# Head-mix matmul as three float32r products for 76 of 180 blocks, with parts made on ScalarE and GpSimd

## The chip, the cores and the metric

One core of a Trainium2 chip runs the whole program. The metric is device time in microseconds, the median of several runs. In the profile PE is TensorE (matmuls; PEld is its weight loads), DVE is VectorE, ACT is ScalarE, POOL is GpSimd and SP is the engine that issues most DMA transfers. Each of them takes its own instructions in the order of the program, and waits only where one needs another's result or buffer.

## What is computed

Attention with two mixings over the heads, then a mixture of experts with one expert per token, then a feed-forward layer. Only the first part is touched by the change:

```python
scores = scale * np.matmul(q, k.transpose(0, 1, 3, 2))      # 4 x 12 x 448 x 448
scores = np.einsum('bhij,hg->bgij', scores, w_pre)          # head mix, 12 x 12
scores = scores - np.max(scores, axis=-1, keepdims=True)
attn = np.exp(scores)
attn = attn / (np.sum(attn, axis=-1, keepdims=True) + 1e-09)
attn = np.einsum('bhij,hg->bgij', attn, w_post)             # second head mix
out = np.matmul(attn, v)
```

All of it is float32. What follows (`_moe_ref`, `_moe2_ref`) reads the attention's output.

## The kernel before

The queries are cut into 16 tiles `T` (four per batch, of 120, 120, 120 and 88 rows). The scores of a tile (function `emit_S`, two head pairs at a time as `emit_S2`) are left in SBUF as `ssb`, rows by query. To mix heads, a matmul must contract over heads, so the tile is cut into 180 blocks in all, of 10 queries x 12 heads = 120 partitions (a few of 8 x 12 = 96). A DMA, `emit_relay`, moves each block from `ssb` into its own tile `sr` (eight buffers), seven steps ahead of its use.

The main loop has one step per block. In step `s` it issues, in this order: the relay for a later block; the head mix of block `s` (`emit_P`: one float32 matmul of 120 x 448 with the block-diagonal weights `wpre`, into PSUM tile `P`, then VectorE's row maximum `mx`); `emit_W(s-1)`, by which VectorE turns the row sum of the block before into the scaled second mix `w`; one "fill" of TensorE (`emit_S2` scores of a coming tile, `emit_AV2` attention times values for a finished one, or transposes); ScalarE's exponential of block `s`, called `ex()`, which writes `p` and the row sum; a conversion step `conv_do` (three VectorE and three GpSimd instructions on a 128 x 256 piece of the feed-forward weights, tiles `ct` and `cm`, and a store) in some steps; and the second mix `emit_T(s-2)`, four float32 matmuls that need both `p` and `w` of block `s-2`, with their copy to `A` by ScalarE. `P` and `T` have two PSUM buffers each. The tables that say which fill falls into which step are fixed when the program is built; the steps with `emit_AV2` come about every fourth.

A float32 value is split elsewhere in this kernel into a high part, rounded to float32r, and a low part, the rest. A product is then three float32r matmuls, high by high, low by high and high by low; `emit_S`, the experts and the feed-forward layer all do this already. The head mix `P` and the second mix `T` are plain float32, which the trace shows as two instructions per matmul.

Of the kernel before, what the change touches and what calls it, by code (L numbers as in the profile page):

```python
# [8 lines left out]
F32 = mybir.dt.float32  # L9
F32R = mybir.dt.float32r  # L10
# [20 lines left out]
def body(ctx: ExitStack, tc, q, k, v, w_pre, w_post, emb, tau, w1, w2, win, wout, out):  # L31
    nc = tc.nc
    pe, act, dve, pool, sp = nc.tensor, nc.scalar, nc.vector, nc.gpsimd, nc.sync
    B, H, S, D = q.shape
# [19 lines left out]
    def ps(tag, nm):  # L54
        if len(PB) > 1:
            tag = {"a": "h", "b": "h"}.get(tag, "o")
        return psum[-1].tile([128, 512], F32, tag=tag, name=nm, bufs=PB[-1][tag])
# [72 lines left out]
    if True:  # L130
        cp = ctx.enter_context(tc.tile_pool(name="route", bufs=1, side="left"))
        aA = actx.enter_context(tc.tile_pool(name="attnA", bufs=1, side="right"))
        a2 = actx.enter_context(tc.tile_pool(name="attnC", bufs=1, side="right"))
        ap = bctx.enter_context(tc.tile_pool(name="attnB", bufs=1, side="left"))

        LAG = 2
        NSR = 8
        taub = cp.tile([128, 1], F32, name="taub")
        nat = {}
# [35 lines left out]
        pool.affine_select(dmask, dmask, pattern=[[-12, 10]], compare_op=ALU.is_ge, fill=0.0, base=0, channel_multiplier=1)  # L175
        pool.affine_select(dmask, dmask, pattern=[[12, 10]], compare_op=ALU.is_ge, fill=0.0, base=11, channel_multiplier=-1)
        wpre = a2.tile([120, 120], F32, name="wpre")
        wpost = a2.tile([120, 120], F32, name="wpost")

        def prep_w():  # L180
            v3 = lambda t, i: t.rearrange("p (a b) -> p a b", b=i)
            mb = dmask.rearrange("p (i o) -> p i o", o=1).to_broadcast([120, 10, H])
            pool.tensor_tensor(v3(wpre, H), mb, wr[:, 0:1, :].to_broadcast([120, 10, H]), op=ALU.mult)
            pool.tensor_tensor(v3(wpost, 10), dmask.rearrange("p (o i) -> p o i", o=1).to_broadcast([120, H, 10]),
                              wr[:, 1, :].rearrange("p (g o) -> p g o", o=1).to_broadcast([120, H, 10]), op=ALU.mult)
# [128 lines left out]
        s_sb = {}  # L314
# [25 lines left out]
        blocks = []  # L340
        for T in range(4 * B):
            n = IT[T % 4][1]
# [6 lines left out]
        NBK = len(blocks)  # L349
# [5 lines left out]
        sr = {}  # L355

        def emit_relay(i):
            T, r, m = blocks[i]
            t = a2.tile([120, S], F32, tag="sr", name=f"sr{i}", bufs=NSR)
            sp.dma_start(t[:12 * m, :], s_sb[T][qsl(T, r, m), :, :])  # L360
            sr[i] = t

        def qsl(T, r, m):
            nb = IT[T % 4][1] // 10
            return slice(r, r + nb * 9 + 1, nb) if r < nb else slice(10 * r, 10 * r + m)

        pj = {}

        def emit_P(i):
            n = 12 * blocks[i][2]  # L370
            t = sr.pop(i)
            pt = ps("b", f"P{i}")
            pe.matmul(pt[:n, :S], wpre[:n, :n], t[:n, :], start=True, stop=True)  # L373

            flush2()
            mx = a2.tile([120, 4], F32, tag="mx", name=f"mx{i}", bufs=5)
            dve.tensor_reduce(mx[:n, 0:1], pt[:n, :S], op=ALU.max, axis=AX.X, negate=True)  # L377
            p = a2.tile([120, S], F32, tag="p", name=f"p{i}", bufs=LAG + 1)
            pj[i] = (p, mx)
            return lambda: act.activation(p[:n, :], pt[:n, :S], AF.Exp, bias=mx[:n, 0:1], scale=1.0, accum_out=mx[:n, 1:2])  # L380
# [261 lines left out]
    with mctx:  # L642
# [321 lines left out]
        def at(pos, fn, *a):  # L964
            side.setdefault(int(pos), []).append((fn, a))
# [3 lines left out]
        def at_e(pos, fn, *a):  # L969
            pos = int(pos)  # L970
            while pos in eused:
                pos += 1
            eused.add(pos)
            at(pos, fn, *a)
            return pos
# [8 lines left out]
        def posAV(T, p):  # L984
            f, nb = first[T + 1], ntile[T + 1]
            return f + LAG + 1 + p * nb / 6

# [48 lines left out]
        kinds = lambda k: [x[0] for x in side.get(k, [])]  # L1036
# [7 lines left out]
        for j, st in enumerate(steps):  # L1044
# [2 lines left out]
            at(ld, conv_load, j, ap)  # L1047
            at(st, conv_do, j, ap)

        nxt = [0]  # L1050

        w1c = []
# [16 lines left out]
        def relay_to(i):  # L1069
            while nxt[0] <= min(i, NBK - 1) and blocks[nxt[0]][0] in sdone:  # L1070
                emit_relay(nxt[0])
                nxt[0] += 1
# [4 lines left out]
        def flush(tag=None):  # L1077
            keep = []
            while late:
                x = late.pop(0)  # L1080
                if tag in (None, x[0]):
                    y = x[1]()
                    if x[0] == "e" and callable(y):
                        late2.append((x[0], y))
                else:
                    keep.append(x)
            late.extend(keep)
            if tag:
                flush2(tag)
# [3 lines left out]
        def flush2(tag=None):  # L1093
            for x in late2[:]:
                if tag in (None, x[0]):
                    late2.remove(x)
                    x[1]()
# [39 lines left out]
        prep_w()  # L1137
        relay_to(NSR - 1)
        at_e(4, tr_en)
# [7 lines left out]
        for _ in pen:  # L1147
            pass
        for s in range(NBK + LAG + 6):
            todo = side.get(s, [])  # L1150
            fill = [x for x in todo if x[0] in PEF]
            for fn, a in todo:
                if fn in (load_q, load_k, load_v, conv_load, zero_fill):
                    fn(*a)
            flush()
            relay_to(s + NSR - 1)
            ex = emit_P(s) if s < NBK else lambda: None
            if 0 <= s - 1 < NBK:
                emit_W(s - 1)
            for fn, a in todo:  # L1160
                if fn is emit_R and a[1] in (0, 1, 3):
                    fn(*a)
            i = s - LAG
            on = 0 <= i < NBK
            fill.sort(key=lambda x: x[0] not in (emit_S, emit_S2, emit_AV2))
            if fill and fill[0][0] in (emit_S, emit_S2, emit_AV2):
                run_fill(*fill.pop(0))
            ex()
            for fn, a in todo:
                if fn is conv_do:  # L1170
                    fn(*a)
            if on:
                emit_T(i)
                T_mm(i, 0, NJ)
                flush("d")
            turns = [x for x in fill if x[0] in (tr_q, tr_k)] if on else []
            for fn, a in turns:
                flush("e")
                late2.append(("e", fn(*a)()))
            if on:  # L1180
                emit_TE(i)
            for x in fill:
                if x not in turns:
                    run_fill(*x)
            for fn, a in todo:
                if fn in (to_experts, first_gather) or fn is emit_R and a[1] in (2, 4, 5, 6):
                    fn(*a)
            for fn, a in todo:
                if fn is do1:
                    fn(*a)  # L1190
        flush()
        flush2()
        for k_ in side:
            assert k_ < NBK + LAG + 6

# [334 lines left out]
    with tc.If(again > 0):  # L1530
# [8 lines left out]
        with tc.tile_pool(name="again", bufs=1, reuse_waits="tile") as gp:  # L1539
            with tc.For_i(0, NT // XT, 1) as tx:  # L1540
# [5 lines left out]
                for j in range(QJ):  # L1546
# [5 lines left out]
                    for hf in range(2):  # L1552
                        pt = ps("c", f"yx{j}_{hf}")
# [7 lines left out]
                with tc.For_i(0, F2 // FG, 1) as gx:  # L1561
# [33 lines left out]
                    for j in range(QJ):  # L1595
                        sl = slice(j * QT, (j + 1) * QT)
                        for n0 in (0, 384):
                            pt = ps("c", f"ox{j}_{n0}")
# [33 lines left out]
```

## Time and profile before

| | us |
|---|---|
| median of 3 runs (1297.14 to 1297.43) | 1297.22 |
| the profiled execution, its own time | 1295.99 |
| its span, first to last instruction | 1294.1 |
| PE busy in the span | 1283.5 |
| DVE busy | 1003.8 |
| ACT busy | 747.7 |
| POOL busy | 489.4 |

The attention loop takes the span's first 500 us or so, the experts and the feed-forward layer the rest. The granted TensorE clock was 1.0 throughout, the upper of the two levels, 2.4 GHz. Times in the rows further down are microseconds from the span's start unless marked ns; in rows of groups, the number after the comma is the mean of one instruction in ns.

### The profile page before, as it was taken

Reading aid. Unit: us, or ns where it says so; the run is one execution under the profiler, and the core shown is the slowest. Engines: PE = TensorE matmul, PEld = TensorE weight load, DVE = VectorE, ACT = ScalarE, POOL = GpSimd, SP = SyncE. Lnnn points to the kernel's source line nnn. Section 1 sums busy time; section 2 is a strip of 40 time slices with the busy share of each in tenths; the row PEclk is TensorE's granted clock in tenths of the full one; section 3 lists DMA queues with packets and bytes.
Section 4 is the critical chain, followed back from the end, with each engine's and each line's share of the span. In section 5 each row is a group of like instructions: output and inputs, shape, how many; then the busy total and the mean of one; then the engine's idle time right before and its main releaser. Section 6 shows DMA issues by size and latency. Waiting matters only on the chain.

```text
span 1294.1 us, 24851 instructions
## 1 busy us (share of the span) xinstructions
PE 1283.5 (99%) x9072; PEld 1125.4 (87%) x9072; DVE 1003.8 (78%) x2168; ACT 747.7 (58%) x1513; POOL 489.4 (38%) x497
## 2 busy tenths in 40 slices
PE   9999999999999999999999999999999999999998
PEld 6777777777777778999999999999999999999997
DVE  5877877787878677788787676788888887888886
ACT  6767666666766665555544545765444556444432
POOL 1334423351344126333223222454644544444431
PEclk9999999999999999999999999999999999999999
DMA  7887665666557458778988876321211123111102
GB/s 172 268 267 214 199 204 152 200 202 192 160 168 223 147 157 301 262 264 250 268 245 259 265 241 210 105 86 49 86 58 65 49 99 122 50 50 49 50 25 88
DMA packets 153077, 210.95 MB, mean 163 GB/s; under 512 B 57686, under 2 KB 113158, under 8 KB 152950
## 3 DMA queue, kind: packets, MB, share of 16 engines
q1 hardware_dynamic: 149680, 195.37, 49.1%
q0 software_dynamic: 2480, 12.19, 2.7%
q8 instruction: 74, 1.21, 0.4%
q10 hardware_dynamic: 790, 1.74, 0.4%
q14 instruction: 53, 0.43, 0.1%
HBM read 135.71 MB, written 35.01 MB: 132 GB/s over the span
## 4 chain that ended last, share of the span: by engine, by line
PE 94%; DVE 2%; DMA 2%; ACT 1%; issue 0%; POOL 0%; SPq 0%; DVEq 0%; POOLq 0%
PE T L412 12%; PE P L373 10%; PE AV L430 6%; PE o L1454 6%; PE o L1452 6%; PE o L1453 6%; PE h L1418 6%; PE h L1417 6%; PE h L1416 6%; PE S L330 5%; PE ypi L706 3%; PE ypi L707 3%; PE ypi L705 3%; PE hi L729 3%; PE hi L730 3%; PE hi L731 3%
## 5 line engine op out<-in xcount | busy, mean ns | idle before, releaser
L412 PEld LDWEIGHTS T<-w,p 120*112 120x112 f32 (+1 forms) x1440 | 166.1, 177 | 59.5 <-issue 46.0
L122 POOL TENSOR_TENSOR cm<-cm,ct 128x256 f32<-128x256 f32 x96 | 70.7, 736 | 313.5 <-DVE ct L119 291.6
L412 PE MATMUL T<-w,p 120*112 120x120 f32 (+1 forms) x1440 | 185.0, 272 | 0.2 <-ACT p L380 0.2
L1399 POOL TENSOR_TENSOR gl<-th,gh 128x512 fp32r<-128x512 f32 (+1 forms) x64 | 77.5, 1211 | 241.1 <-ACT gh L1398 180.4
L373 PE MATMUL P<-sr,wpre 120*120 120x448 f32 x360 | 166.3, 544 | 1.0 <-DMA sr<-ssb 1.0
L380 ACT ACTIVATE p<-P,mx 120x448 f32<-120x448 f32 x180 | 114.1, 634 | 89.9 <-DVE mx L387 76.2
L1420 ACT ACTIVATE u<-h 128x512 f32<-128x512 f32 (+1 forms) x64 | 35.0, 547 | 204.1 <-PE h L1418 204.1
L1452 PE MATMUL o<-woh,gh 128*128 128x384 f32 x448 | 151.4, 338 | 0.0
L1454 PE MATMUL o<-woh,gl 128*128 128x384 f32 x448 | 150.4, 336 | 0.0
L1453 PE MATMUL o<-wol,gh 128*128 128x384 f32 x448 | 150.1, 335 | 0.0
L1458 DVE TENSOR_TENSOR acc<-acc,o 128x384 f32<-128x384 f32 x196 | 106.5, 548 | 47.2 <-PE o L1454 47.2
L377 DVE TENSOR_REDUCE mx<-P 120x1 f32<-120x448 f32 x180 | 111.6, 620 | 28.9 <-PE P L373 26.7
L120 POOL TENSOR_TENSOR cm<-craw 128x256 f32<-128x256 f32 x96 | 66.9, 697 | 112.8 <-DMA craw<-in_moe_w_in 59.2
L417 ACT COPY A<-T 112x480 f32<-112x480 f32 x180 | 102.3, 568 | 9.7 <-PE T L412 9.7
L729 PE MATMUL hi<-xhi,w1h 128*128 128x256 f32 x336 | 95.3, 283 | 0.0
L730 PE MATMUL hi<-xli,w1h 128*128 128x256 f32 x336 | 95.2, 283 | 0.0
L731 PE MATMUL hi<-xhi,w1l 128*128 128x256 f32 x336 | 95.2, 283 | 0.0
L705 PE MATMUL ypi<-w2hi,hhi 128*128 128x384 f32 x272 | 93.9, 345 | 0.0
L430 PEld LDWEIGHTS AV<-A,v 112*64 112x64 f32 x1536 | 73.9, 137 | 21.8 <-issue 10.7
L706 PE MATMUL ypi<-w2li,hhi 128*128 128x384 f32 x272 | 91.2, 335 | 0.2 <-DVE w2li L673 0.2
L707 PE MATMUL ypi<-w2hi,hli 128*128 128x384 f32 x272 | 91.2, 335 | 0.0
L121 POOL TENSOR_SCALAR cm<-cm 128x256 f32<-128x256 f32 x96 | 85.9, 895 | 8.4
(299 smaller groups left out, 3436.3 us busy)
## 6 DMA issues: line engine op xcount, KB each, us to landing
sr<-ssb SPq DMA_DIRECT2D x176, 210.0 KB
r<-in_moe_w SPq DMA_DIRECT2D x72, 384.0 KB
r<-in_moe_w SPq DMA_DIRECT2D x52, 512.0 KB
craw<-in_moe_w_in SPq DMA_DIRECT2D x48, 256.0 KB
craw<-in_moe_w_out SPq DMA_DIRECT2D x48, 256.0 KB
wor<-wo_d SPq DMA_DIRECT2D x16, 768.0 KB
raw<-wi_d SPq DMA_DIRECT2D x15, 768.0 KB
wi_d<-cm SPq DMA_DIRECT2D x48, 128.0 KB
```

What stands on the lines that cost most here:

```text
L373: pe.matmul(pt[:n, :S], wpre[:n, :n], t[:n, :], start=True, stop=True)
L412: pe.matmul(pt[:CP, c * n:(c + 1) * n] if m == 10 else pv[:, c], p[:n, c * CP:(c + 1) * CP], w[:n, :] if m == 10 else wv, start=True, stop ...
L430: pe.matmul(pt[64 * hh:64 * hh + 64, x * 120:x * 120 + n], vt[b, p + x][:, hh, c, :], A[T][:, c, 2 * (p + x) + hh, :n], start=c == 0, stop ...
L705: pe.matmul(pt[:, :384], a, wh[:, n0:n0 + 384], start=f == 0, stop=False)
L706: pe.matmul(pt[:, :384], a, wl[:, n0:n0 + 384], start=False, stop=False)
L707: pe.matmul(pt[:, :384], l, wh[:, n0:n0 + 384], start=False, stop=f == KF - 1)
L729: pe.matmul(pt[:, :256], wh[:, sl], xh[:, c, :], start=c == 0, stop=False)
L730: pe.matmul(pt[:, :256], wh[:, sl], xl[:, c, :], start=False, stop=False)
L731: pe.matmul(pt[:, :256], wl[:, sl], xh[:, c, :], start=False, stop=c == KD - 1)
L1452: pe.matmul(pt[:, :384], gh[:, sl], wo[0][:, f, n0:n0 + 384], start=f == 0, stop=False)
L1453: pe.matmul(pt[:, :384], gh[:, sl], wo[1][:, f, n0:n0 + 384], start=False, stop=False)
L1454: pe.matmul(pt[:, :384], gl[:, sl], wo[0][:, f, n0:n0 + 384], start=False, stop=f == GF - 1)
```

## The change

Steps with an `emit_AV2` fill (41 of them between step 12 and step 168) prepare blocks `s+2` and `s+3`; if the step also holds scores, `s+2` alone. That is 35 steps with two blocks and 6 with one, 76 blocks of 180. Preparing a block (`split_sr`) is one ScalarE copy of `sr` (120 x 448) into a new float32r tile `sh` with three buffers, the high part, and one GpSimd subtraction that leaves the low part in `sr`. The weights are split once, in step 2, by two VectorE instructions (`split_w`). The head mix of a prepared block is then three float32r products; the other 104 stay as they were. Nothing else is altered.

```diff
+        AHEAD = 2
...
+        wprs = [a2.tile([120, 120], F32R, name=f"wpr{t}") for t in "hl"]
...
-            t = a2.tile([120, S], F32, tag="sr", name=f"sr{i}", bufs=NSR)
-            sp.dma_start(t[:12 * m, :], s_sb[T][qsl(T, r, m), :, :])
+            t = a2.tile([120, S], F32R, tag="sr", name=f"sr{i}", bufs=NSR)
+            sp.dma_start(t.bitcast(F32)[:12 * m, :], s_sb[T][qsl(T, r, m), :, :])
...
+        def split_w():
+            dve.tensor_copy(wprs[0], wpre)
+            dve.tensor_sub(wprs[1], wpre, wprs[0].bitcast(F32))
+
+        def split_sr(i):
+            n = 12 * blocks[i][2]
+            sh[i] = ap.tile([120, S], F32R, tag="sh", name=f"sh{i}", bufs=3)
+            act.copy(sh[i][:n, :], sr[i].bitcast(F32)[:n, :])
+            pool.tensor_sub(sr[i][:n, :], sr[i].bitcast(F32)[:n, :], sh[i].bitcast(F32)[:n, :])
...
-            t = sr.pop(i)
+            t, h = sr.pop(i), sh.pop(i, None)
             pt = ps("b", f"P{i}")
-            pe.matmul(pt[:n, :S], wpre[:n, :n], t[:n, :], start=True, stop=True)
+            if h is None:
+                pe.matmul(pt[:n, :S], wpre[:n, :n], t.bitcast(F32)[:n, :], start=True, stop=True)
+            else:
+                pe.matmul(pt[:n, :S], wprs[0][:n, :n], h[:n, :], start=True, stop=False)
+                pe.matmul(pt[:n, :S], wprs[1][:n, :n], h[:n, :], start=False, stop=False)
+                pe.matmul(pt[:n, :S], wprs[0][:n, :n], t[:n, :], start=False, stop=True)
...
+        splits = {k: [k + AHEAD, k + AHEAD + 1][:1 if emit_S2 in kinds(k) else 2] for k in range(12, NBK - 11) if emit_AV2 in kinds(k)}
...
             ex()
+            if s == 2:
+                split_w()
+            for j in splits.get(s, ()):
+                split_sr(j)
             for fn, a in todo:
                 if fn is conv_do:
                     fn(*a)
```

The text ahead of the prediction and the prediction itself use step 90 as the example, an `emit_AV2` step without scores and with two conversions. ScalarE's instructions there before, from the exponential of block 90 (`p`) on (`xT` is the copy of the attention output, `A` that of `T`, `ssb` that of scores):

```order
L380 ACTIVATE p_3695,mx_3693<-P_3690,mx_3693 120x448
L432 COPY xT_3485<-AV_4_3700 128x240
L417 COPY A_3465<-T_3736 112x48x10
L337 ACTIVATE ssb_3590<-S_2_3756 120x896
L334 ACTIVATE ssb_3590<-S_3_0_3763 120x448
L380 ACTIVATE p_3751,mx_3749<-P_3747,mx_3749 120x448
```

And of the change, at the same place:

```order
L398 ACTIVATE p_3879,mx_3877<-P_3874,mx_3877 120x448
L379 CAST sh_3902<-sr_3704 120x448
L379 CAST sh_3905<-sr_3733 120x448
L450 COPY xT_3654<-AV_4_3884 128x240
L435 COPY A_3634<-T_3926 112x48x10
L339 ACTIVATE ssb_3769<-S_2_3946 120x896
L336 ACTIVATE ssb_3769<-S_3_0_3953 120x448
L398 ACTIVATE p_3941,mx_3939<-P_3937,mx_3939 120x448
```

Two copies, of blocks 92 and 93, now stand between the exponential and everything that ScalarE does next.

GpSimd's instructions before, from the end of an earlier conversion through the two of step 90 (`craw` is the loaded piece, `ct` what VectorE makes of it):

```order
L122 TENSOR_TENSOR cm_3611<-cm_3611,ct_3610 128x256
L120 TENSOR_TENSOR cm_3719<-craw_3554 128x256
L121 TENSOR_SCALAR cm_3719<-cm_3719 128x256
L122 TENSOR_TENSOR cm_3719<-cm_3719,ct_3718 128x256
L120 TENSOR_TENSOR cm_3728<-craw_3556 128x256
L121 TENSOR_SCALAR cm_3728<-cm_3728 128x256
L122 TENSOR_TENSOR cm_3728<-cm_3728,ct_3727 128x256
```

And of the change:

```order
L122 TENSOR_TENSOR cm_3793<-cm_3793,ct_3792 128x256
L380 TENSOR_TENSOR sr_3704<-sr_3704,sh_3902 120x448
L380 TENSOR_TENSOR sr_3733<-sr_3733,sh_3905 120x448
L120 TENSOR_TENSOR cm_3909<-craw_3729 128x256
L121 TENSOR_SCALAR cm_3909<-cm_3909 128x256
L122 TENSOR_TENSOR cm_3909<-cm_3909,ct_3908 128x256
L120 TENSOR_TENSOR cm_3918<-craw_3731 128x256
L121 TENSOR_SCALAR cm_3918<-cm_3918 128x256
L122 TENSOR_TENSOR cm_3918<-cm_3918,ct_3917 128x256
```

The two subtractions stand ahead of all six instructions of the two conversions. Before, GpSimd took the first two of a conversion as soon as its piece was loaded, and then waited for VectorE's `ct`; now they are behind the subtractions.

VectorE's order is the same in both but for the two instructions of `split_w`, and so is SP's.

## Rows read from the trace of the kernel before

**Rows 1.** The page's busy times, and its chain that ended last, by line.
```profile
PE 1283.5 (99%) x9072; PEld 1125.4 (87%) x9072; DVE 1003.8 (78%) x2168; ACT 747.7 (58%) x1513; POOL 489.4 (38%) x497
...
PE T L412 12%; PE P L373 10%; PE AV L430 6%; PE o L1454 6%; PE o L1452 6%; PE o L1453 6%; PE h L1418 6%; PE h L1417 6%; PE h L1416 6%; PE S L330 5%; PE ypi L706 3%; PE ypi L707 3%; PE ypi L705 3%; PE hi L729 3%; PE hi L730 3%; PE hi L731 3%
```

**Rows 2.** Busy us of PE, PEld, DVE, ACT, POOL in one stretch of the loop.
```profile
200.00:300.00 100.00, 100.00 (x879) 74.82 (x878) 78.59 (x233) 69.63 (x166) 41.34 (x57) 1.00 0.60 182
```

**Rows 3.** Chain of waits, steps 87 to 95: start, time held, what.
```profile
255.85 0.86 PE T L412 x8
...
260.57 0.75 PE P L373 x2
261.32 1.40 PE S L330 x12
...
264.45 0.82 PE T L412 x8
...
271.36 0.75 PE P L373 x2
...
273.52 1.01 PE T L412 x8
```

**Rows 4.** The same view where float32r products follow each other, 384 and 512 columns.
```profile
511.39 0.23 PE hoi0a L747
...
569.11 0.17 PE ypi L705
```

**Rows 5.** Groups by line and shape, ScalarE, 200 to 300 us.
```profile
L293 ACT CAST kh<-ptk 128x448 fp32r<-128x448 f32 x5 | 2.6, 527 | 2.0 <-PE ptk L287 2.0
```

**Rows 6.** The same view of GpSimd, 200 to 300 us; the last from 900 us on.
```profile
L121 POOL TENSOR_SCALAR cm<-cm 128x256 f32<-128x256 f32 x19 | 16.3, 856 | 1.7
L122 POOL TENSOR_TENSOR cm<-cm,ct 128x256 f32<-128x256 f32 x19 | 13.8, 728 | 61.1 <-DVE ct L119 54.5 <-DMA v<-in_v 6.4
L120 POOL TENSOR_TENSOR cm<-craw 128x256 f32<-128x256 f32 x19 | 12.0, 632 | 0.6 <-DMA craw<-in_moe_w_in 0.6
...
L1399 POOL TENSOR_TENSOR gl<-th,gh 128x384 fp32r<-128x384 f32 x27 | 28.9, 1072 | 113.8 <-ACT gh L1398 69.1 <-issue 39.8 <-PE o L1454 4.9
```

**Rows 7.** Timeline of VectorE in steps 90 and 91: start, duration.
```profile
259.57 0.42 DVE L118 SCALAR_TENSOR_TENSOR ct<-craw,ct 128x256 int32<-128x256 int32 x1
260.03 0.42 DVE L119 SCALAR_TENSOR_TENSOR ct<-craw,ct 128x256 int32<-128x256 int32 x1
...
260.69 0.92 DVE L118 SCALAR_TENSOR_TENSOR ct<-craw,ct 128x256 int32<-128x256 int32 x1
261.64 0.72 DVE L119 SCALAR_TENSOR_TENSOR ct<-craw,ct 128x256 int32<-128x256 int32 x1
262.29 0.61 DVE L377 TENSOR_REDUCE mx<-P 120x1 f32<-120x448 f32 x1
...
263.19 0.77 DVE L390 TENSOR_SCALAR w<-wpost,mx 120x120 f32<-120x120 f32 x1
```

**Rows 8.** Timeline of GpSimd over the same steps.
```profile
260.60 0.73 POOL L122 TENSOR_TENSOR cm<-cm,ct 128x256 f32<-128x256 f32 x1 [5.87 <-DVE ct L119]
261.29 0.80 POOL L120 TENSOR_TENSOR cm<-craw 128x256 f32<-128x256 f32 x1
```

**Rows 9.** Timeline of ScalarE, steps 87, 90 and 93.
```profile
251.73 0.21 ACT L380 ACTIVATION_READ_ACCUMULATOR p<-P,mx 120x1 f32 x1
...
259.40 0.19 ACT L380 ACTIVATION_READ_ACCUMULATOR p<-P,mx 120x1 f32 x1
...
269.25 0.19 ACT L380 ACTIVATION_READ_ACCUMULATOR p<-P,mx 120x1 f32 x1
```

**Rows 10.** Timeline of VectorE: second mix's weights of block 87, and of block 93.
```profile
255.24 0.28 DVE L390 TENSOR_SCALAR w<-wpost,mx 120x120 f32<-120x120 f32 x1
...
271.53 0.33 DVE L390 TENSOR_SCALAR w<-wpost,mx 120x120 f32<-120x120 f32 x1
```

**Rows 11.** The tile `sr`: idle time of engines before its instructions, by what ended it.
```profile
  DMA sr<-ssb: 1.5, 2
```

More of the change, by code (lines that the diff above doesn't have):

```diff
@@ L367, in body @@
         pj = {}
+        sh = {}
+        def split_w():
[6 more added lines that the diff above has]
+            pool.tensor_sub(sr[i][:n, :], sr[i].bitcast(F32)[:n, :], sh[i].bitcast(F32)[:n, :])
         def emit_P(i):
             n = 12 * blocks[i][2]
-            t = sr.pop(i)
+            t, h = sr.pop(i), sh.pop(i, None)
             pt = ps("b", f"P{i}")
-            pe.matmul(pt[:n, :S], wpre[:n, :n], t[:n, :], start=True, stop=True)
+            if h is None:
[4 more added lines that the diff above has]
+                pe.matmul(pt[:n, :S], wprs[0][:n, :n], t[:n, :], start=False, stop=True)
             flush2()
```

## Prediction

> **What bounds the kernel now.** I read the page first. TensorE is busy for 1283.5 of 1294.1 us, and the sixteen lines that hold most of the chain that ended last are all its matmuls: the head mix, line 373, with 10%, the second mix, line 412, with 12% [rows 1]. A busy TensorE need not be the limit, so I looked at one stretch of the attention loop: 100.00 of 100 us on TensorE, 78.59 on VectorE, 69.63 on ScalarE, 41.34 on GpSimd [rows 2]. The chain of waits there runs from matmul group to matmul group with no other engine between them [rows 3]. So time taken off TensorE in the loop ends the program earlier, as long as nothing that TensorE waits for comes later; and VectorE has only some 21% to spare.
>
> **Gain on TensorE.** A float32 head mix holds the chain for 0.75 us [rows 3]. What a full-height float32r product of 448 columns takes is not in the trace, but its neighbours are: 0.17 us for 384 columns and 0.23 for 512, each following another [rows 4]. Halfway between them, 448 columns take 0.20, three products 0.60, and the gain is 0.15 us a block. With 76 blocks that is 11.4 us. The bounds: scaled by columns from the 384-column row a product takes 0.198, so 0.16 a block and 12 us in all; at worst it goes like the score products, also float32r and 448 columns, but in pairs on half the rows: 1.40 us for six pairs, 0.233 each [rows 3], 0.70 a block, a gain of 0.05 and 3.8 us. I take 0.20, since the head mix's 120 rows are close to the full-height rows and it is not done in pairs.
>
> **Added work, ScalarE.** The nearest copy, 128 x 448 into float32r, takes 527 ns [rows 5], so two add 1.05 us in a step, 40 us in all. In step 90 the row sum ends at 259.59 (259.40 + 0.19) [rows 9]; the copies end near 260.7, and the next large work, the copies of the scores, can start only after the score products that begin at 261.32 [rows 3]. In between lie two copies of about half a microsecond; they end a little later than before, and the two new ones fit. They wait for the relay DMAs too, three steps earlier than the matmul did; with relays issued seven steps ahead and only two waits for them in the whole program, 1.5 us together [rows 11], I cost this at nothing. If relays were late by one step, ScalarE and then TensorE would stop for it.
>
> **Added work, GpSimd.** Subtractions of 256 and 384 columns take 728 and 1072 ns [rows 6]; on that line 448 columns take 1.24 us; the longer one was itself measured beside a busier VectorE, so I take 1.15, 87 us in all. GpSimd has room for it (41.34 us in 100 [rows 2]). For its deadline I take step 93, where the row sum ends at 269.44 [rows 9] and block 95's head mix starts at 271.36 [rows 3]: copy until 269.97, subtraction until 271.12. That is 0.24 us early, and only the third product needs it, 0.40 later. So the subtraction itself holds nobody up unless VectorE holds it up.
>
> **What the subtraction does to VectorE.** This is the term that can eat the gain. In step 90 the two-tensor instructions of line 118 and 119 take 0.42 us while GpSimd is idle; the same two take 0.92 and 0.72 when GpSimd's instruction, begun at 260.60, and its successor at 261.29 run beside them, and the latter takes 0.80 instead of 0.61 to 0.63 [rows 6 to 8]. So does line 390, the weights `w` of the second mix: 0.28 alone [rows 10], 0.77 at 263.19 [rows 7]. One engine waits for the other, about 0.5 us an encounter behind a GpSimd instruction of 0.73.
>
> The Trainium skill says so too (SBUF — State Buffer, "SBUF: two separate sides"): VectorE instructions with two SBUF inputs, or in a two-port mode, and GpSimd's exclude each other for a whole instruction. The 0.92 us row agrees. By that rule a subtraction of 1.15 us could hold VectorE for up to 1.15, not 0.5, an encounter; that speaks against the change.
>
> Where does it reach TensorE? Through `w`, which matmul `T` needs two steps on. Step 90: line 118's second run, at 260.69, meets the first subtraction, which can run from 260.46 (after line 119) until 261.6, and line 119's second run meets the other one, until 262.8. The conversions end near 263.1, not 262.36 (261.64 + 0.72) [rows 7]; maximum and `w` follow 0.7 us late, so `w` is ready at 264.7, not 263.96. `T` of block 90 starts at 264.45 [rows 3], now 0.15 earlier because block 92 is faster: the wait is about 0.4, and to 1.0 if GpSimd's line 121, 856 ns [rows 6], is in front of `w` as well. I take 0.7, at steps 45, 90 and 135, which are alike: 2.1 us. Step 87: the row sum ends at 251.94 [rows 9], copy until 252.47, subtraction until 253.6, and the conversion's three GpSimd instructions (0.632, 0.856 and 0.728 [rows 6]), of which two ran long before, follow until 255.9. They cover `w` at 255.24 [rows 10], so it ends at 256.0, not 255.52; `T` starts at 255.85 [rows 3], less 0.15: 0.3 to 0.5 late. I take 0.4, at steps 42, 87 and 132: 1.2 us. Elsewhere there is more room: `w` of block 93 is ready at 271.86 [rows 10] and its matmul starts at 273.52 [rows 3], so 1.6 us of delay would be hidden, and most of the other steps look like that; for the odd ones, such as the two steps with two conversions at either end of the loop, I add 0.9. Together 4.2 us of new waits; without any cover of that kind each of the 76 subtractions would cost its 0.5 us, 38 us.
>
> **Sum.** 11.4 - 4.2 = 7.2 us off the profiled execution's 1295.99 us, that is 1288.8. The median was 1297.22, 1.2 above that execution, so I forecast 1290.0. The two instructions that split the weights come once, in step 2, and are below 1 us on VectorE; SP's order is unchanged, and the experts behind the loop just start earlier.
>
> **Rivals.**
> - *No new wait.* For: GpSimd is idle for more than half of the stretch [rows 2], so encounters may simply be spread over slack. Against: line 390's 0.77 us right before a `T` that needs it. Time: 1297.2 - 11.4 = 1285.8.
> - *Waits in more steps.* Each of the 76 subtractions holds VectorE once for 0.5 us, 38 us, and 27% of that, 10.3 us, comes through to TensorE instead of the 11% that I count (4.2 of 38). Time: 1296.1. For: VectorE's 78.59 us in 100 [rows 2] becomes 85 or more.
> - *VectorE becomes the bound of the steps with `emit_AV2`, and the kernel slower.* The same mechanism with 40% coming through, 15.2 us: 1301.0. It decides from 11.4 of 38, 30%, on. By the rule of the skill cited above the holds are up to 1.15 us, 87 us in all, and 13% would be enough. Against: in step 90 an encounter cost 0.5, and the 1.6 us of block 93 is the commoner slack.
> - *The products aren't faster.* At the 0.233 of the score pairs the gain is 3.8, less 4.2 of waits: 1297.6. Against: both full-height rows [rows 4].
>
> **Numbers.** Chances: forecast 0.48 (its own range 1287 to 1293), no new wait 0.27, waits in more steps 0.14, slower 0.07, products not faster 0.04. A measurement tells 0.2%, 2.6 us, from no change. Faster, below 1294.6: the first two and a third of the third, 0.79; slower, above 1299.8: 0.08, with a little from the last; same: 0.13. The range from 1285.0 to 1296.0 holds the first two, with a gain up to 12 us, and half of the third.
>
> **What would show it.** The head mix's pieces in the chain at 0.58 to 0.62 us for 76 blocks and 0.75 for 104; ScalarE's copies near 0.53 and GpSimd's subtractions at 1.1 to 1.3; line 118, 119 and `w` groups with a higher mean; new waits of `T` for `w` at steps 42, 45, 87, 90, 132 and 135, and few elsewhere; hardly any wait for the subtraction or the relays. I am wrong if TensorE's waits in the loop pass some 6 us, or if a block's three products hold the chain for other than 0.6 us.

## The result, and the profile after

| | before | changed |
|---|---|---|
| median of 6 runs each, us | 1297.33 (1295.62 to 1297.82) | 1308.24 (1306.48 to 1311.47) |
| the profiled execution, its own time | 1295.99 | 1308.34 |
| its span | 1294.1 | 1306.5 |

The ratio is 1.0081, with an interval of 1.0067 to 1.0095: the change makes the kernel slower by 0.8%, where a gain of 7 us was forecast. The page of the changed kernel answers to [rows 1]; these are its busy times and its chain that ended last, by engine and by line:

```profile
PE 1281.1 (98%) x9148; PEld 1139.6 (87%) x9148; DVE 1013.0 (78%) x2170; ACT 778.5 (60%) x1589; POOL 585.7 (45%) x573
...
PE 82%; DVE 8%; DMA 4%; ACT 3%; issue 1%; POOL 1%; SPq 0%; POOLq 0%; DVEq 0%; ACTq 0%
PE T L430 8%; PE o L1478 6%; PE o L1476 6%; PE o L1477 6%; PE h L1442 6%; PE h L1441 6%; PE h L1440 6%; PE AV L448 4%; PE P L387 4%; PE S L332 4%; PE ypi L724 3%; PE ypi L725 3%; PE ypi L723 3%; PE hi L747 3%; PE hi L749 3%; PE hi L748 3%
```

TensorE's busy time fell, by 2.4 us, and the program still became longer. In [rows 1] the second mix `T` was 12% and the head mix 10% of that chain; here `T` is 8%, the plain head mixes are 4%, and 8% of the chain runs over VectorE. Before it was 2%:

```profile
PE 94%; DVE 2%; DMA 2%; ACT 1%; issue 0%; POOL 0%; SPq 0%; DVEq 0%; POOLq 0%
```

The windows of the loop, before and then after (length, busy us of PE, PEld, DVE, ACT, POOL, clock, DMA share, GB/s), say how far:

```profile
20.00:492.00 472.00, 472.00 (x4091) 351.57 (x4090) 361.26 (x1114) 322.07 (x767) 161.16 (x221) 1.00 0.66 201
```

```profile
20.00:502.00 482.00, 468.99 (x4165) 365.45 (x4163) 371.48 (x1116) 352.66 (x843) 256.56 (x298) 1.00 0.64 195
200.00:300.00 100.00, 98.36 (x875) 76.73 (x871) 76.83 (x226) 74.91 (x179) 62.40 (x73) 1.00 0.62 183
```

TensorE was never idle in the loop and now is for 13.0 us, at the same granted clock of 1.00. The line of 200 to 300 us answers to [rows 2]: 98.36 us in place of 100.00. What ended TensorE's waits between 20 and 510 us (us in total, times, longest; before, this view had 1.0 us for a relay and 0.2 us for `p`):

```profile
PE T L430 <- ACT A L435: 4.4, 3, 2.6
PE T L430 <- DVE w L408: 4.4, 8, 1.1
PE T L430 <- ACT qh L312: 1.1, 1, 1.1
PE P L387 <- DMA sr<-ssb: 1.0, 1, 1.0
...
PE P L391 <- POOL sr L380: 0.3, 1, 0.3
```

Relays and the subtraction itself keep TensorE hardly at all (1.0 us, as before, and 0.3). It is `T` that waits. The view names `w`, ScalarE's copy `A` and `qh` as what ended the waits; the rows around step 45 below show that it was `w` nearly every time.

**The book of the 12.4 us of span.** I compared the starts of the same block's head mix in both traces. Where nothing waits, a prepared block's way from `T` to `T` takes 0.717 us instead of 0.856, 0.139 less; 76 blocks give 10.6. The last head mix of the loop nevertheless starts at 502.9 and not 492.6. Up to block 175 the loop is 6.95 us longer, so 17.5 us of new delay stand against the 10.6; blocks 175 to 179 add 3.30; what is behind the loop adds 2.15. The sum, 6.95 + 3.30 + 2.15, is 12.4. Of the 20.8 us of new delay in the loop 13.0 are idle time in the windows; the rest does not show as idle time in this profile, in which the ends of matmuls are modelled.

**The products** are as forecast. The chain of waits near the end of the loop (start, time held, what) has the three of one prepared block and then a plain one:

```profile
476.00 0.21 PE P L389
476.20 0.20 PE P L390
476.40 0.20 PE P L391
...
477.61 0.75 PE P L387 x2
```

0.61 us in place of the 0.75 of [rows 3].

**Where VectorE loses it.** Around step 45, GpSimd and then VectorE, by start and duration:

```profile
140.25 2.50 POOL L380 TENSOR_TENSOR sr<-sr,sh 120x448 fp32r<-120x448 f32 x2 [4.52 <-ACT sh L379]
...
144.58 0.72 POOL L122 TENSOR_TENSOR cm<-cm,ct 128x256 f32<-128x256 f32 x1
```

```profile
139.38 0.28 DVE L117 TENSOR_SCALAR ct<-craw 128x256 int32<-128x256 int32 x1
139.70 0.43 DVE L118 SCALAR_TENSOR_TENSOR ct<-craw,ct 128x256 int32<-128x256 int32 x1
...
140.50 1.23 DVE L117 TENSOR_SCALAR ct<-craw 128x256 int32<-128x256 int32 x1
141.77 1.26 DVE L118 SCALAR_TENSOR_TENSOR ct<-craw,ct 128x256 int32<-128x256 int32 x1
143.07 0.72 DVE L119 SCALAR_TENSOR_TENSOR ct<-craw,ct 128x256 int32<-128x256 int32 x1
143.71 0.61 DVE L395 TENSOR_REDUCE mx<-P 120x1 f32<-120x448 f32 x1
...
144.62 0.76 DVE L408 TENSOR_SCALAR w<-wpost,mx 120x120 f32<-120x120 f32 x1
```

The first conversion is done alone: lines 117 and 118 take 0.28 and 0.43 us. The second one meets two subtractions: line 117 takes 1.23 and line 118 takes 1.26. Then the row maximum can start only at 143.71, though its head mix is long done, and `w` comes behind it. Before, from the second conversion of the same step on:

```profile
136.64 0.29 DVE L117 TENSOR_SCALAR ct<-craw 128x256 int32<-128x256 int32 x1
136.96 0.92 DVE L118 SCALAR_TENSOR_TENSOR ct<-craw,ct 128x256 int32<-128x256 int32 x1
...
138.56 0.61 DVE L377 TENSOR_REDUCE mx<-P 120x1 f32<-120x448 f32 x1
...
139.47 0.77 DVE L390 TENSOR_SCALAR w<-wpost,mx 120x120 f32<-120x120 f32 x1
```

From the start of the second line 117 to the end of `w` it was 3.60 us and is now 4.88. The long `w` itself, beside GpSimd's line 122, is not new. ScalarE, TensorE's weight load and its matmul then are:

```profile
145.04 0.47 ACT L435 COPY A<-T 112x384 f32<-112x384 f32 x1
```

```profile
145.49 0.27 PEld L430 LDWEIGHTS T<-w,p 120*112 120x112 f32 x2 [1.28 <-ACT p L398]
```

```profile
145.52 1.05 PE L430 MATMUL T<-w,p 120*112 120x120 f32 x8 [0.93 <-ACT A L435]
```

The view puts this wait of 0.93 us down to the copy `A`. But the weight load of the same `T` began at 145.49, before that copy ended at 145.51, so the copy did not release it; `w` had ended at 145.38. The same holds for the wait of 0.90 at 394.91, also put down to `A`. In all eleven waits of `T` up to 467 us, whatever the view names, `T` starts 0.14 to 0.15 us behind the end of `w`; they are 7.4 us together. Only the one at 499.54, 2.6 us, ends later, 0.24 us behind `w` and 0.05 behind a copy `A`. So maximum late, `w` late, `T` late: 10.0 of the 13.0 us of idle time.

I call a hold what an instruction of VectorE takes beyond its usual duration (the lower quartile of its form) where that is over 0.1 us and a GpSimd instruction was running as it began. In the loop of before the holds come to 22.6 us, after to 35.2. Of these, 14.9 us are 20 holds by the subtraction, 0.75 us each, the longest 0.95.

The Trainium skill (SBUF — State Buffer, "SBUF: two separate sides") says that one of the two engines takes the shared port for its whole instruction and the other stops. The trace agrees: the two subtractions, one row above, end at 141.59 and 142.75; line 117, begun at 140.50, ends at 141.73, 0.14 behind the first, and line 118, begun at 141.77, ends at 143.03, 0.28 behind the second. Each waited for the whole rest of an instruction. The Trainium skill limits this on VectorE's side to instructions with two SBUF inputs or in a two-port mode, and counts `tensor_scalar`, which line 117 is, among those that can run in one. Line 117 has one input; in which mode it ran no row here shows.

**Where the end of the loop loses it.** SP's queue (start, duration, count), before:

```profile
466.70 0.93 SPq L123 DMA_DIRECT2D wo_d<-cm  x1
467.74 8.85 SPq L360 DMA_DIRECT2D sr<-ssb  x6
...
481.44 2.46 SPq L939 DMA_DIRECT2D r<-in_moe_w  x5
```

and after:

```profile
471.81 2.55 SPq L362 DMA_DIRECT2D sr<-ssb  x3
478.11 0.34 SPq L123 DMA_DIRECT2D wo_d<-cm  x1
478.55 7.66 SPq L362 DMA_DIRECT2D sr<-ssb  x6
...
493.35 2.29 SPq L957 DMA_DIRECT2D r<-in_moe_w  x5
```

The store of a converted piece, line 123, stands in SP's order ahead of the last six relays and waits until 478.11 for GpSimd's line 122. GpSimd did two subtractions, at 473.31 for 2.46 us, ahead of that conversion. So SP, which had issued the three relays before at 474.36, stands still for 3.75 us. The chain of waits goes on from there:

```profile
484.51 8.79 DMA sr<-ssb
...
493.35 3.61 DMA r<-in_moe_w
...
496.98 0.70 DVE w1h L687
497.68 0.53 DVE mx L395
```

SP waits for the last relay before it loads the experts' weights. Their conversion `w1h` (line 687) stands in VectorE's order ahead of the row maximum of one of the last blocks, so `mx` and `w` wait for expert weights, and `T` with them: 499.54, after 2.6 us.

### The profile page after: what moved, and what is told of

Same layout as the page of the kernel before. It is cut to its first block, busy times and chain, and to the rows that moved or that the text cites. A ratio compares the mean times of both kernels' runs of the same rounds, so it can differ in the third digit from the quotient of the medians.

```text
span 1306.5 us, 25214 instructions
## 1 busy us (share of the span) xinstructions
PE 1281.1 (98%) x9148; PEld 1139.6 (87%) x9148; DVE 1013.0 (78%) x2170; ACT 778.5 (60%) x1589; POOL 585.7 (45%) x573
## 4 chain that ended last, share of the span: by engine, by line
PE 82%; DVE 8%; DMA 4%; ACT 3%; issue 1%; POOL 1%; SPq 0%; POOLq 0%; DVEq 0%; ACTq 0%
PE T L430 8%; PE o L1478 6%; PE o L1476 6%; PE o L1477 6%; PE h L1442 6%; PE h L1441 6%; PE h L1440 6%; PE AV L448 4%; PE P L387 4%; PE S L332 4%; PE ypi L724 3%; PE ypi L725 3%; PE ypi L723 3%; PE hi L747 3%; PE hi L749 3%; PE hi L748 3%
## 5 line engine op out<-in xcount | busy, mean ns | idle before, releaser
L380 POOL TENSOR_TENSOR sr<-sr,sh 120x448 fp32r<-120x448 f32 x76 | 92.1, 1230 | 142.5 <-ACT sh L379 113.4
L387 PE MATMUL P<-sr,wpre 120*120 120x448 f32 x208 | 96.5, 546 | 1.0 <-DMA sr<-ssb 1.0
L448 PEld LDWEIGHTS AV<-A,v 112*64 112x64 f32 x1536 | 73.9, 137 | 20.8 <-issue 9.7
```

Source lines behind the costliest of these rows:

```text
L387: pe.matmul(pt[:n, :S], wpre[:n, :n], t.bitcast(F32)[:n, :], start=True, stop=True)
L448: pe.matmul(pt[64 * hh:64 * hh + 64, x * 120:x * 120 + n], vt[b, p + x][:, hh, c, :], A[T][:, c, 2 * (p + x) + hh, :n], start=c == 0, stop ...
```

## The experiments

Theory H throughout: the loss is GpSimd's subtraction, by way of VectorE, which is held while it runs. The rivals have their letters in the expectations. Diffs are against the changed kernel. "Loop" is the start of a block's head mix against before, up to block 175, where the changed kernel has +6.95. Each is read from one profiled execution. The first head mix of these traces lies 0.40 us earlier to 0.64 us later than before's; counted from its own first head mix the changed kernel has +7.05, and run 3, in which TensorE does what it did before, +0.07.

**1. No subtraction, the products kept.** It leaves out the low part: the third product takes `sh` again.

```diff
-            pool.tensor_sub(sr[i][:n, :], sr[i].bitcast(F32)[:n, :], sh[i].bitcast(F32)[:n, :])
...
-                pe.matmul(pt[:n, :S], wprs[0][:n, :n], t[:n, :], start=False, stop=True)
+                pe.matmul(pt[:n, :S], wprs[0][:n, :n], h[:n, :], start=False, stop=True)
```

> The 76 GpSimd subtractions are left out; the third product takes the high part a second time, so the head mix of these blocks lacks its low part, and TensorE does the same work. Theory H (GpSimd's subtractions, and the conversions pushed behind them, hold VectorE, and the second mix's weights come late): 1286 to 1288.5 us, that is the gain of 11.4 us with hardly a new wait. Theory S (ScalarE's two copies per step push the exponentials and copies behind them): little changes, 1304 to 1308 us.

1289.56 us, ratio 0.9940 (0.9924 to 0.9957). Loop -8.4, blocks 175 to 179 +0.68. The products and ScalarE's copies are there, and with them 8.4 of the 10.6 us of gain; the time is a little above H's bounds. Most of the loss in the loop, 15.4 us, hangs on the subtraction; the other 2.2 us do not come through even without it.

**2. Copies and subtractions, no products.** The results of the preparation are not used; every head mix is plain float32.

```diff
-            pool.tensor_sub(sr[i][:n, :], sr[i].bitcast(F32)[:n, :], sh[i].bitcast(F32)[:n, :])
+            pool.tensor_sub(sh[i][:n, :], sr[i].bitcast(F32)[:n, :], sh[i].bitcast(F32)[:n, :])
...
-            if h is None:
-                pe.matmul(pt[:n, :S], wpre[:n, :n], t.bitcast(F32)[:n, :], start=True, stop=True)
-            else:
-                pe.matmul(pt[:n, :S], wprs[0][:n, :n], h[:n, :], start=True, stop=False)
-                pe.matmul(pt[:n, :S], wprs[1][:n, :n], h[:n, :], start=False, stop=False)
-                pe.matmul(pt[:n, :S], wprs[0][:n, :n], t[:n, :], start=False, stop=True)
+            pe.matmul(pt[:n, :S], wpre[:n, :n], t.bitcast(F32)[:n, :], start=True, stop=True)
```

> Copies and subtractions as in the change, but the subtraction's result goes into the copy's tile and is not used: every head mix stays one float32 matmul. Both theories put the whole loss here and no gain: 1312 to 1320 us. If the time is below 1303, most of the loss comes only with the faster products, that is from the shorter room for everything else.

1312.50 us, ratio 1.0114 (1.0088 to 1.0140). The price of the preparation alone: its loop ends 14.3 us late, 3.13 of it in blocks 175 to 179. The 11.2 up to block 175 are less than the 17.5 of the changed kernel, so a part of its delay arises only beside the shorter head mixes.

**3. Copies alone**, without the subtraction, and with the plain head mixes of run 2.

```diff
-            pool.tensor_sub(sr[i][:n, :], sr[i].bitcast(F32)[:n, :], sh[i].bitcast(F32)[:n, :])
```

> Only ScalarE's 76 copies are added, no subtraction, all head mixes float32. Theory H: 1296.5 to 1299 us, as before the change. Theory S: 1306 us or more.

1297.23 us, ratio 0.9998 (0.9988 to 1.0009). ScalarE's 76 copies cost nothing, as the prediction had it.

**4. The subtraction on VectorE.**

```diff
-            pool.tensor_sub(sr[i][:n, :], sr[i].bitcast(F32)[:n, :], sh[i].bitcast(F32)[:n, :])
+            dve.tensor_sub(sr[i][:n, :], sr[i].bitcast(F32)[:n, :], sh[i].bitcast(F32)[:n, :])
```

> The change with the subtraction on VectorE instead of GpSimd, 76 times some 0.5 us. Theory H: VectorE is busy for 0.5 us instead of being held for 0.9 to 1.2, and GpSimd's conversions are not pushed back: 1289 to 1298 us, clearly below the change. Theory S: 1305 to 1309 us.

1322.29 us, ratio 1.0182 (1.0165 to 1.0199): slower than either theory. I had thought of its duration alone. What VectorE stood idle for in the loop (first row), and the instruction's own duration (min, median, max):

```profile
DVE sr L380 <- ACT sh L379: 29.7, 40, 1.2
```

```profile
L380 DVE TENSOR_TENSOR sr<-sr,sh x76: 615/623/627, 53.2 to 489.4; 120x448 fp32r<-120x448 f32 x73, 96x448 fp32r<-96x448 f32 x3
```

It takes 0.62 us, but in its place in the order it waits for ScalarE's copy, 40 times and 29.7 us in all, and conversion, maximum and `w` wait behind it. H's time for this run was wrong with that. The run does not decide on H, since it makes VectorE late for another reason; it shows that VectorE's lateness reaches TensorE: the loop ended 24.2 us late.

**5. Half the subtraction**, 224 of 448 columns; the low part of the others is left out.

```diff
-            pool.tensor_sub(sr[i][:n, :], sr[i].bitcast(F32)[:n, :], sh[i].bitcast(F32)[:n, :])
+            pool.tensor_sub(sr[i][:n, :S // 2], sr[i].bitcast(F32)[:n, :S // 2], sh[i].bitcast(F32)[:n, :S // 2])
```

> The subtraction covers 224 of the 448 columns, so the right half of these blocks' third product reads the unsplit scores. Theory H (GpSimd holds VectorE for the length of its instruction, behind which the chain to the second mix is late): a hold about half as long, and half of the 18.6 us between the run without subtractions and the change: 1296 to 1301 us. Rival W (it is the number of GpSimd instructions and their waits, or the conversions queued behind them, not how long each one runs): 1304 to 1308 us.

The total, 2658 us, can't be used: with the altered values some 9800 instructions run behind 1290 us that the other kernels do not run. In the loop: -2.67, between -8.4 without subtraction and +6.95 with it. Of the 15.4 us between, 5.7 are left, 37% (35% when each is counted from its own first head mix), with the same number of subtractions. The holds by them fall to 5.5 us (14 of them). The length of the instruction counts, not how many there are. It does not separate a hold from a conversion that is late in GpSimd's queue, for that queue is shorter here too.

**6. Only calm steps**: 17 steps, 34 blocks, those in which the trace of the changed kernel shows no loss over 0.2 us.

```diff
-        splits = {k: [k + AHEAD, k + AHEAD + 1][:1 if emit_S2 in kinds(k) else 2] for k in range(12, NBK - 11) if emit_AV2 in kinds(k)}
+        splits = {k: [k + AHEAD, k + AHEAD + 1][:1 if emit_S2 in kinds(k) else 2] for k in range(12, NBK - 11) if emit_AV2 in kinds(k) and 6 < k % 45 < 30 and 45 < k < 160}
```

> The change in 17 of its 41 steps, 52 to 72, 97 to 117 and 142 to 158, 34 blocks, where its trace shows few new waits. Theory H: 34 times 0.14 us of gain, 4.7, less about 1.5 of waits: 1293.5 to 1295.5 us, faster than before the change. Rival W: the loss goes with the number of subtractions, 34 of 76 of the 10.9 us, so 1300 to 1304 us.

1296.58 us, ratio 0.9976 (0.9959 to 0.9992). The loop is 3.61 us shorter, of 34 x 0.139 = 4.7 possible, and TensorE has no new wait (1.0 us for a relay and 0.2 for `p`, as before). There were 6 holds by the subtraction, 2.0 us in all. It is the one version here that leaves nothing out and beats before, by 0.24%; with an interval from 0.08 to 0.41% that is a small gain, and the loop is the firmer sign. In its profiled execution 5.1 us are lost behind the loop, 2.0 of them at the token gather (below). Another 2.9 are lost at a second gather: TensorE waits 1.89 us for `yg` until 803.95, in place of 0.48 before, and then its granted clock falls to 0.50:

```profile
805.00:808.40 3.40, 3.40 (x16) 3.40 (x15) 1.11 (x2) 1.69 (x3) 2.77 (x4) 0.50 0.89 301
```

Runs 4 and 8 have the same wait (2.11 and 2.45 us) with the same fall behind it. Why `yg` lands late in them was not tested.

**7. Without the last two preparing steps**, 4 blocks fewer.

```diff
-        splits = {k: [k + AHEAD, k + AHEAD + 1][:1 if emit_S2 in kinds(k) else 2] for k in range(12, NBK - 11) if emit_AV2 in kinds(k)}
+        splits = {k: [k + AHEAD, k + AHEAD + 1][:1 if emit_S2 in kinds(k) else 2] for k in range(12, NBK - 11) if emit_AV2 in kinds(k) and k < 160}
```

> The change without the preparations in steps 162 and 166, 4 blocks less. Theory E (at the loop's end a conversion's store waits on SP for GpSimd, the last relays behind it land late, and the first expert's weights after them): the 3.3 us lost in the last four steps come back, with 1 us in steps 160 to 175 less 0.6 of gain: 1303 to 1305 us. Rival L (the weights are late because the new tiles moved buffers in memory, whenever relays are issued): 1307 to 1309 us.

1305.19 us, ratio 1.0061 (1.0040 to 1.0082). Blocks 175 to 179: 0.00 in place of +3.30, and 160 to 166 gives 0.86 us back as well. Its SP queue at the end of the loop is again as before:

```profile
472.18 0.92 SPq L123 DMA_DIRECT2D wo_d<-cm  x1
473.20 8.97 SPq L362 DMA_DIRECT2D sr<-ssb  x6
```

So the loss at the end is that of the store waiting for GpSimd behind those subtractions. Run 4, whose subtraction is on VectorE, loses nothing there either; run 1, which has none, loses 0.68.

**8. Preparation in other steps**, partly steps with scores. These are 28 blocks; the expectation counts 30.

```diff
-        splits = {k: [k + AHEAD, k + AHEAD + 1][:1 if emit_S2 in kinds(k) else 2] for k in range(12, NBK - 11) if emit_AV2 in kinds(k)}
+        splits = {k: [k + AHEAD, k + AHEAD + 1][:2 if emit_AV2 in kinds(k) else 1] for k in range(60, 160) if k % 45 in (15, 17, 19, 21, 23, 27)}
```

> 30 blocks, in steps 60 to 72 and the same places 45 and 90 steps on, where hardly any conversion runs; two score steps of each stretch prepare one block too. Theory H: 30 times 0.14, 4.2 us, nearly all kept: 1293 to 1294.5 us. Rival W: 30 of 76 of the 10.9 us lost: 1300 to 1303 us.

1297.81 us, ratio 1.0001 (0.9981 to 1.0020), a miss. The loop gains 0.94 us of 28 x 0.139 = 3.9: in score steps ScalarE's copies of `ssb` stand ahead of `sh`, and now the third product does wait for the subtraction:

```profile
PE P L391 <- POOL sr L380: 1.1, 4, 0.3
```

**9 and 10. Conversions one step later**, in 9 with preparation before step 160 as in run 7, in 10 with none, as the control.

```diff
+        steps = sorted(k + 1 if emit_AV2 in kinds(k) and k + 1 not in routed and emit_AV2 not in kinds(k + 1) and k < 160 else k for k in steps)
```

> The change without the blocks prepared at the end (steps from 160 on), and the weight conversion of a preparing step done one step later, so that GpSimd's subtractions run while VectorE has no conversion in front of it. Theory H (a VectorE instruction is held by the subtraction that runs beside it, and most of the held ones are those of the conversions, lines 117 to 119): fewer than 10 instructions of VectorE held by the subtraction, in place of 20, TensorE's new waits in the loop at most a third of those of the change, and 1291 to 1297 us. Theory W (the subtractions take GpSimd's time, and the conversions behind them in its queue are late whatever VectorE does): the waits stay, 1303 to 1307 us, like the change without its end, 1305.19.

> The control: conversions one step later as in the run beside it, but no block prepared, all head mixes plain float32. Both theories: 1296 to 1299 us, as before. If the moved conversions cost or gain something by themselves, it is seen here, and the other run is read against this one.

1331.04 us, ratio 1.0256 (1.0235 to 1.0277), and 1320.96, ratio 1.0188 (1.0166 to 1.0211). Both theories missed both. The control alone loses 24 us: moved by one step, the conversions are, as I read its order, in front of other work of VectorE. The subtraction held VectorE in 8 places for 3.0 us instead of 14.0 in run 7, and yet run 9 is 10 us behind its control, and 15.4 in the profiled executions. A part of that has another cause. Its windows behind a wait of 2.46 us of `T`, which starts at 108.59:

```profile
110.00:111.00 1.00, 1.00 (x5) 0.80 (x4) 0.23 (x1) 0.76 (x3) 0.00 (x0) 0.50 0.54 156
111.00:112.00 1.00, 1.00 (x2) 0.00 (x0) 0.62 (x1) 0.71 (x2) 0.00 (x0) 0.50 0.87 228
112.00:113.00 1.00, 1.00 (x7) 0.82 (x8) 0.75 (x3) 0.00 (x0) 0.00 (x0) 0.70 0.57 198
```

The granted clock fell from 1.00 (2.4 GHz) to 0.50 (1.2 GHz) after it, and a float32 head mix took 1.71 us there. In the same place the control had a wait of 2.02 us and kept 1.00. It fell six times in the loop of run 9 and never in the control's. Over the span the mean clock of the profiled executions was 0.992 against 0.999; 0.007 of 1329 us is some 9 us, an estimate, of their 15.4. The control's other executions had 0.993 to 0.997, so between the medians the clock explains less. These two runs can't decide between the theories.

**11 and 12. The subtraction in two and in four pieces**, otherwise as run 7; nothing is left out. The diff is that of 11; in 12 the 224 is 112.

```diff
-            pool.tensor_sub(sr[i][:n, :], sr[i].bitcast(F32)[:n, :], sh[i].bitcast(F32)[:n, :])
+            for c in range(0, S, 224):
+                pool.tensor_sub(sr[i][:n, c:c + 224], sr[i].bitcast(F32)[:n, c:c + 224], sh[i].bitcast(F32)[:n, c:c + 224])
```

> The change without the blocks prepared at the end, with each subtraction cut into two of 224 columns; the same values, nothing left out. GpSimd's time stays about as it is (it grows nearly with the columns: 256 take 728 ns and 384 take 1072). Theory H (VectorE is held for the rest of the one GpSimd instruction that it meets): the longest hold goes from about 0.95 to about 0.5 us, the loop loses about half of what it lost, and 1297 to 1302 us against 1305.19 of the uncut kernel. Theory W (what counts is GpSimd's time in all, or the work queued behind it): 1304 to 1307 us, as uncut.

> The same with each subtraction cut into four of 112 columns, nothing left out. Theory H: a hold is at most about 0.3 us, though one VectorE instruction after another can meet a piece; 1292 to 1300 us, and no longer than the two pieces. Theory W: 1304 to 1309 us, with the cost of the added instructions on GpSimd on top.

1301.78 us, ratio 1.0028 (1.0015 to 1.0041), and 1306.02, ratio 1.0055 (1.0041 to 1.0069). The first total looks like H, but isn't: counted from its own first head mix, the loop of run 11 is 5.5 us longer than before's, that of run 7 5.7, and that of run 12 10.2. The profiled executions of 7 and 11 lie 4.1 us apart, and that arises behind the loop. GpSimd's pieces (min, median, max of their durations), of 11 and of 12:

```profile
L381 POOL TENSOR_TENSOR sr<-sr,sh x144: 647/666/948, 53.2 to 451.7; 120x224 fp32r<-120x224 f32 x138, 96x224 fp32r<-96x224 f32 x6
```

```profile
L381 POOL TENSOR_TENSOR sr<-sr,sh x288: 408/425/715, 53.3 to 457.4; 120x112 fp32r<-120x112 f32 x138, 96x112 fp32r<-96x112 f32 x6
```

A hold does become shorter: 19 of 0.74 us in run 7, 35 of 0.36 in 11, 40 of 0.20 in 12. But a block's subtraction grows from 1.155 us to 1.33 and 1.70, and TensorE's weight loads wait for it (1.2 us in run 7, 3.1 in 11, 6.0 in 12). And GpSimd is late with its conversions: VectorE's line 117 has to wait for GpSimd's line 122, never before, 0.6 us in the changed kernel and in run 7, 4.1 in 11 and 8.8 in 12. The rows are of the changed kernel and of run 12:

```profile
DVE ct L117 <- POOL cm L122: 0.6, 1, 0.6
```

```profile
DVE ct L117 <- POOL cm L122: 8.8, 4, 2.7
```

Shorter pieces trade one wait for another. What they add is the way of theory W, late conversions; in the changed kernel that way is 0.6 us.

## Why the prediction was wrong

*Gain on TensorE*: right. A block's products hold the chain for 0.61 us (forecast 0.60), and 76 blocks give 10.6 us (11.4).

*Added work, ScalarE*: right, nothing (run 3), though a copy takes 0.56 us and not 0.53.

*Added work, GpSimd*: its size was nearly right, 1.16 us in the median and 1.23 in the mean for 1.15, 92 us in all for 87. That it holds up nobody itself is right as well for the third product, 0.3 us. But it was counted with the conversions of the step only for VectorE's sake. GpSimd's end was also the start of a store.

*What the subtraction does to VectorE*: the step that failed. The sum had 4.2 us of new waits, "11% of 38 us"; up to block 175 there are 17.5. Taken apart, as what single steps lose net of their own gain (those over 0.2 us, 12.0 us in 20 steps; the other 5.5 are small delays and gains that don't come through):
- The six steps worked out in it do lose, and somewhat more than forecast. "0.7" behind each of steps 45, 90 and 135 was 0.98, 0.69 and 0.95 (in steps 47, 93 and 137); "0.4" behind 42, 87 and 132 was 0.55, 0.55 and 0.56 (in 44, 89 and 134). Together 4.28 us for 3.3.
- "Elsewhere there is more room", with 0.9 us for odd steps such as the two with two conversions: this is the term that was wrong. The steps at the two ends of the loop lose 2.0 us (17: 0.79, 164: 1.01, 168: 0.20), and eleven that I had not looked at 5.7 more, the most in 24 to 37 (0.70, 0.41, 0.31, 0.88, 1.16, 0.25), the rest in 79, 82, 95, 124 and 127. The room of block 93, 1.6 us, was taken for the usual one; "most of the other steps look like that" was not read step by step.
- An encounter costs 0.75 us in the mean, up to 0.95, not "about 0.5". The 0.5 was read from [rows 6 to 8], behind a GpSimd instruction of 0.73. Behind one of 1.16 it is longer, as the rule of the Trainium skill cited in the prediction would have it; run 5 halves the instruction and 37% of the loss is left. Line 117, with one input, was not counted among those held.
- Only 20 of the 76 subtractions meet VectorE in that way. But what they take passes on: the holds grow by 12.6 us (35.2 - 22.6), and the loop loses more than that, not the 11% that was counted.
- The way that was followed, from `w` to `T`, was right: 10.0 of TensorE's 13.0 us of idle time end behind `w`, 2.6 of them at the end of the loop. What failed is the number of steps in which it leads to a wait, and the size of an encounter.

*"SP's order is unchanged, and the experts behind the loop just start earlier"*: wrong. An unchanged order is what does the harm: a store that waits for GpSimd holds six relays behind it. 3.30 us, which run 7 gives back. That term was missing from the sum.

*Behind the loop* 2.15 us are lost, and TensorE has a new wait of 1.9: it waits for the gather of an expert's tokens, which GpSimd can issue only when the last of the attention's outputs are stored. Before, GpSimd waited there for the row numbers `ids` (8.0 us); now it waits for that store:

```profile
522.84 1.75 POOL L696 DMA_INDIRECT xgi<-x_d,ids  x1 [9.31 <-DMA x_d<-raw]
```

The last store is issued at 517.25, and GpSimd goes on 5.6 us later; before, it was issued at 507.00, and at 510.8 GpSimd waited for `ids` alone. The same loss is in the traces of runs 1, 4, 6, 7 and 8 (1.3 to 2.3 us), 0.6 of it in 9, and nothing in 2, 3, 10, 11 and 12. Run 1 has no subtraction, so this does not hang on it. Why the store lands late in some I did not find out and did not test.

*The rivals.* What happened is the mechanism of the third, VectorE as the limit of the preparing steps. Its time, 1301.0, lay 3.8 us above before; the profiled executions differ by 12.35. It let 15.2 us through, and 17.5 came (2.3); the end of the loop (3.3) and what is behind it (2.15) were not in it, and the gain was 0.8 less. Its chance was too low: of the two rows held against it, the encounter of 0.5 us belonged to a shorter instruction, and the room of block 93 was not the usual one.

What stays open is how the 17.5 us divide between the holds themselves and the order behind them. Run 1 shows that 15.4 of them come with the subtractions, run 3 that they don't come from the copies alone, run 5 that the subtractions' length counts. That it goes by way of VectorE's held instructions is read from the timelines: VectorE hardly waits for a late conversion (0.6 us), and its holds by others than the subtraction did not grow (22.6 us before, 20.3 after). No run shows it by itself; the two attempts to take the holds away and leave the work (9, and 11 with 12) each brought a cost of their own.

## What to carry to other kernels

VectorE was busy for 77% of this loop and still had little to give, since its idle time lay in gaps of its own. Price an added instruction beside it by its whole duration at each instruction that it can stop there, and ask in every step, not in one, how much of that the bound engine has room for. Where a view names what ended a wait, compare the ends of all that the instruction needs before building on the name. Look at each wait in a DMA queue for an engine that gets new work, and name the transfers behind it. Then place such work by the trace, step by step: 34 of the 76 blocks, in calm steps, turned a loss of 0.8% into a small gain, 0.24%.

## What the runs showed of the hardware

- A VectorE instruction with a single SBUF input, line 117, is held by a GpSimd subtraction as much as one with two: 0.28 us became 1.23. In the traces without that subtraction (before, 1 and 3) it never took more than 0.71.
- GpSimd's two-input subtraction on 120 rows has a fixed part: 1.155, 0.666 and 0.425 us for 448, 224 and 112 columns, so 2.15 ns a column and some 0.18 us on top, an estimate from the last two.
- Three float32r products of 448 columns on 120 rows run at 0.20 us each in the chain, against 0.75 for the float32 pair.
- In run 9 six waits of TensorE (2.46 us three times, 1.98, 2.01, 2.24) were each followed by some 3 us at half clock; the control's of 1.94 to 2.02 us were not, nor was the changed kernel's of 2.62 at 499.54. In run 6 one of 1.89 was. The length of the wait alone does not tell.
